# Dilated and sliding attention into a squared-ReLU layer: when keys, queries and values are turned and copied on the way to the next row

## The chip, the cores and the metric

The kernel runs on one core of one Trainium2 chip. The metric is the device time of one execution in microseconds (us), lower is better. Before the change it is 310.36 us, the median of three runs (309.91 to 311.45).

The engines that matter: PE (matrix multiplies; PEld are its weight loads), DVE (vector), ACT (activations and copies), POOL (casts, and one queue that issues transfers), SP (a queue that only issues transfers). Each engine, and each issuing queue, takes its instructions in program order; they meet through semaphores.

## The reference

`B, H, S, D = 8, 8, 576, 64`. Attention over 8 batch rows, 4 heads with a sliding window of 32, 4 heads with a dilated window (32 keys, every fourth), then a two-layer network with relu squared:

```python
    scores = scale * np.matmul(q, k.transpose(0, 1, 3, 2))
    mask_plain = (rel >= 0) & (rel < window)
    mask_dil = (rel >= 0) & (rel < window * dilation) & (rel % dilation == 0)
    attn = softmax of scores under the mask of the head
    x = np.matmul(attn, v) as (B * S, H * D)
    h = x @ w_in          # 4608 x 512 by 512 x 2048
    g = maximum(h, 0) ** 2
    out = g @ w_out       # 2048 x 512, float32
```

## The kernel before

Everything is in float16 on chip with float32 sums. The 4608 tokens are 8 batch rows of 576 (the attention's unit, called row b below) and 9 chunks of 512 (the network's unit, called chunk c). All order is written out by hand (`tc.manual_schedule()`): an engine executes in the order in which the Python code emits.

**The network as filler.** `moe_gen(c)` is a generator; each `yield` stands after a few matmuls. `mm1_gen` makes 16 tiles `ph` of `x @ w_in` (four matmuls of 512 columns each, line 298), ACT takes relu into `rt` (line 321), DVE squares into `g` (line 322). For chunks above 1, `sum_of_g` (lines 331, 332) and line 406 prepare sums and differences of `g` on DVE, and `mm2_strassen_gen` does the second product with seven half-size products instead of eight. Its bank `A` (tile `pa`) is used four times in turn; after each use ACT copies it out (`take`, line 391), and the next product into `A` has to wait for that copy. Outputs leave by SP (line 397). `pump(n)` advances the generator by n yields, so the attention code of row b, with `pump` between its steps, is woven into the matmuls of chunk b-1.

**Attention of one row.** `attn_scores` makes scores of the sliding heads (`s_sliding`, tiles `ps`, from `QKTp`) and of the dilated heads (`s_dilated`, tiles `pz`, from `QKTd`), with exp on ACT (line 563) and the mask on DVE (line 564). `av_sliding` (tiles `pav`, three steps `mp`) multiplies with the values `vp`, `av_dilated` (tiles `paw`, steps t, a) with `vd`; DVE normalizes into `xs` and `xd` (lines 605, 610). The result goes transposed into `xT`: for rows 0 to 3 by PE and ACT (`x_sliding`, `x_dilated`, lines 657, 675); for rows 4 to 7 (`attn_values_by_dma`) by transposing transfers on SP: `xT<-xs` (line 680), and `yd<-xd` (line 687, t = 0 and 1, called yd_0 and yd_1 here) which ACT then copies into `xT` (line 675, `x_from`).

**What row b+1 needs, made during row b.**
- sliding q and k: loaded by POOL into `ns` (line 112); DVE copies them into token order, `nr` (line 120); SP writes `nr` to DRAM as `dp` (line 217, two halves); SP transposes `dp` into `QKTp` (line 225, k first, then q). `turn` is `nr` and `dp` together.
- dilated q and k: POOL writes them to DRAM as `dd` (line 207); SP transposes into `QKTd` (line 229).
- values: SP loads `sv` (sliding, line 132) and `sd` (dilated, line 137); POOL casts them into `vp` (line 169) and `vd` (line 177).
- the overlap: blocks of values need the tail of the block before in their first partitions. `halo_sliding` (line 184) and `halo_dilated` (line 189) do it on ACT for rows 0 to 2; `halo_sliding_by_dma` (line 194) and `halo_dilated_by_dma` (line 197) do it on SP for rows 3 to 7. The name in the profile is `vp<-vp` and `vd<-vd`.
- `after_transposes` (line 235, tile `seen`) holds POOL's loads for the row after until the last transpose has landed; line 893 does the same with yd_1 ahead of the casts into `vp`.

**The loops.** Row 0 runs alone, with matmuls whose result nobody reads (`fill_gen`, line 507) in its waits; it ends at line 814. Row 1 runs inside the second product of chunk 0 (lines 820 to 836). Then `for b in range(2, 4)` (line 842) and `for b in range(4, B)` (line 867).

Of the kernel before, what the change touches and what calls it, by code (L numbers as in the profile page):

```python
# [17 lines left out]
def kernel(  # L18
# [106 lines left out]
    def load_sliding_v(b):  # L125
        vv = v[b, 0:HH].rearrange("h (m p) d -> p h m d", p=QB)
        if b == 0:
            for m in range(NB):
                nc.sync.dma_start(out=sv[PADP:P, :, m, :], in_=vv[:, :, m, :])
        else:  # L130
            for h in (0, 2):
                nc.sync.dma_start(out=sv[PADP:P, h : h + 2], in_=vv[:, h : h + 2])  # L132

    def load_dilated_v(b, eng):
        vv = v[b, HH:H].rearrange("h (i c) d -> i h (c d)", c=DIL)
        for t in range(2):
            eng.dma_start(out=sd[P - QD[t] : P, t, :, :], in_=vv[Q0D[t] : Q0D[t] + QD[t]])  # L137
# [55 lines left out]
    def halo_sliding_by_dma(b):  # L193
        nc.sync.dma_start(out=vp[b % 2][0:PADP, 1:NB], in_=vp[b % 2][P - PADP : P, 0 : NB - 1])
# [4 lines left out]
    def cast_v(b):  # L199
        cast_sliding_v(b)  # L200
        cast_dilated_v(b)
# [22 lines left out]
        for i in (1, 0):  # L224
            nc.sync.dma_start_transpose(out=QKTp[b % 2][:, i, :, PADP:], in_=dp[i])

    def transpose_dilated(b, dd):
        for i in (1, 0):
            nc.sync.dma_start_transpose(out=QKTd[b % 2][:, i, :, KPAD:], in_=dd[i])


# [271 lines left out]
    def fill_gen():  # L503
        for n in range(1000):
# [2 lines left out]
                nc.tensor.matmul(pf, ident, maskp[:, 0:TOKC], start=True, stop=True)  # L507
            yield

    pending: list = []  # L510

    def pump(n):
        for _ in range(n):
            while pending:
                try:
                    next(pending[0])
                    break
                except StopIteration:
                    pending.pop(0)
# [142 lines left out]
    def x_dilated(b, t, xs, wide):  # L662
        py = pt(f"py{b}_{t}", wide)
        w = QD[t]
        for r in range(DIL):
            x = xs[1][t][:, r].rearrange("p h d -> p (h d)")
            for c in range(2):
                o = w * (2 * r + c)
                nc.tensor.transpose(py[:, o : o + w], x[:, P * c : P * (c + 1)], ident[0:w, 0:w])
        x_from(b, t, py[:, 0 : 8 * w].rearrange("x (r c i) -> x r c i", r=DIL, c=2))  # L670
# [14 lines left out]
    def x_dilated_by_dma(b, t, xs):  # L685
        y = yp.tile([P, DIL, 2, QD[t]], FP16, name=f"yd{b}_{t}", tag=f"yd{t}")
        nc.sync.dma_start_transpose(
            out=y.rearrange("x r c i -> x (r c) i"), in_=xs[1][t].rearrange("p r h d -> p (r h d)")
        )
        return y  # L690

    def attn_scores(b, gap, less=0, hooks={}):
        for hp in range(2):
            s_sliding(b, hp)
            if hp in hooks:
                hooks[hp]()
            pump(gap)
        for g in range(2):
            s_dilated(b, g)
            if 2 + g in hooks:  # L700
                hooks[2 + g]()
            if g and b < 3:
                halo_sliding(b, 0)
            pump(gap - less)

    def attn_values(b, gap, wide=False, then=None):
        xs = x_tiles(b)
        for mp in range(3):
            av_sliding(b, mp, xs)
            if b < 3:  # L710
                if mp < 2:
                    halo_sliding(b, mp + 1)
                else:
                    halo_dilated(b, 0)
            if then and b == 2 and mp == 2:
                then()
            pump(gap)
        x_sliding(b, 0, xs, wide)
        if b < 3:
            halo_dilated(b, 2)  # L720
        pump(gap)
        av_dilated(b, 0, 0, xs)
        if then and b == 1:
            then()
        pump(gap)
        x_sliding(b, 1, xs, wide)
        pump(gap)
        av_dilated(b, 0, 1, xs)
        pump(gap)
        for a in range(2):  # L730
            av_dilated(b, 1, a, xs)
            pump(gap)
        x_dilated(b, 0, xs, wide)
        pump(gap)
        x_dilated(b, 1, xs, wide)

    def attn_values_by_dma(b, then):
        xs = x_tiles(b)
        for mp in range(3):
            av_sliding(b, mp, xs)  # L740
            if mp == 1:
                then[0]()
            pump(3)
        x_sliding_by_dma(b, xs)
        ys = []
        for t in range(2):
            for a in range(2):
                av_dilated(b, t, a, xs)
                pump(4 + 2 * (a > t))
            ys.append(x_dilated_by_dma(b, t, xs))  # L750
            then[1 + t](ys[t])
        pump(6)
        x_from(b, 0, ys[0])
        pump(7)
        x_from(b, 1, ys[1])
# [55 lines left out]
    av_dilated(0, 1, 1, xs)  # L811
    begun.append(mm1_begin(0, 1))
    x_dilated(0, 0, xs, False)
    x_dilated(0, 1, xs, False)


    g0 = hidden(0)
# [8 lines left out]
    for a in range(2):  # L826
        t_dilated(1, m, a, True)
        pump(2)
    attn_scores(1, 2, 1)
    dp = []  # L830
    attn_values(1, 1, True, lambda: dp.append(keep_sliding_qk(2, by_token(2, ns))))
    pump(1000)
# [2 lines left out]
    leave_first()  # L835
    load_v(2)


    def turn(b, n):
        return keep_sliding_qk(b, by_token(b, n))  # L840

    for b in range(2, 4):
        pending.append(moe_gen(b - 1))
        nxt = b + 1
        after_transposes(b)
        ns = load_sliding_qk(nxt)
        if b == 2:
            cast_v(b)
        dd = keep_dilated_qk(nxt)
        if b == 3:  # L850
            halo_sliding_by_dma(b)
            halo_dilated_by_dma(b)

        def turn_and_load():
            dp = turn(nxt, ns)
            load_sliding_v(nxt)
            load_dilated_v(nxt, nc.sync)
            transpose_sliding(nxt, dp)
            transpose_dilated(nxt, dd)
            cast_v(nxt)  # L860

        pump(22 if b == 2 else 12)
        attn_scores(b, 4, 0, {3: turn_and_load} if b == 3 else {})
        attn_values(b, b, False, turn_and_load)
        pump(1000)

    for b in range(4, B):
        pending.append(moe_gen(b - 1))
        nxt = b + 1
        if nxt < B:  # L870
            after_transposes(b)
            ns = load_sliding_qk(nxt)
            dd = keep_dilated_qk(nxt)
        if b > 4:
            cast_dilated_v(b)
        halo_sliding_by_dma(b)
        halo_dilated_by_dma(b)
        dps = []

        def copied():  # L880
            if nxt < B:
                dps.append(turn(nxt, ns))

        def first(y):
            if nxt < B:
                load_sliding_v(nxt)

        def second(y):
            if nxt < B:
                transpose_sliding(nxt, dps[0])  # L890
                transpose_dilated(nxt, dd)
                load_dilated_v(nxt, nc.sync)
                nc.gpsimd.tensor_copy(seen, y[:, 0, 0, 0:1])
                cast_sliding_v(nxt)

        pump(3)
        attn_scores(b, 3)
        attn_values_by_dma(b, (copied, first, second))
        pump(1000)
# [33 lines left out]
```

## Time and profile before

| | |
|---|---|
| runs, median of 3 | 310.36 us |
| the profiled execution | 309.19 us, of which 307.1 us lie between its first and last instruction (the span) |
| granted TensorE clock | 1.000 |
| PE busy | 286.5 us (93% of the span), 2762 matmuls |
| PE weight loads | 192.4 us (63%) |
| DVE | 210.1 us (68%) |
| ACT | 172.9 us (56%) |
| POOL | 64.2 us (21%) |
| SP's and ACT's transfer queue (q1) | 68832 packets, 32.96 MB, 51.9% of 16 engines' span |
| POOL's transfer queue (q0) | 8752 packets, 13.63 MB, 26.1% |

PE is busy nearly throughout, so the time is the matmuls plus PE's waits. A row of the timeline gives start, duration, engine, line, operation, and the number of instructions merged. `SPq` means the queue of SP issuing a transfer; the row's duration is that of the issue, and the landing is another, later time.

### The profile page before, as it was taken

Reading aid. Unit: us, or ns where it says so; the run is one execution under the profiler, and the core shown is the slowest. Engines: PE = TensorE matmul, PEld = TensorE weight load, DVE = VectorE, ACT = ScalarE, POOL = GpSimd, SP = SyncE. Lnnn points to the kernel's source line nnn. Section 1 sums busy time; section 2 is a strip of 40 time slices with the busy share of each in tenths; the row PEclk is TensorE's granted clock in tenths of the full one; section 3 lists DMA queues with packets and bytes.
Section 4 is the critical chain, followed back from the end, with each engine's and each line's share of the span. In section 5 each row is a group of like instructions: output and inputs, shape, how many; then the busy total and the mean of one; then the engine's idle time right before and its main releaser. Section 6 shows DMA issues by size and latency. Waiting matters only on the chain.

```text
span 307.1 us, 6899 instructions
## 1 busy us (share of the span) xinstructions
PE 286.5 (93%) x2762; PEld 192.4 (63%) x2762; DVE 210.1 (68%) x434; ACT 172.9 (56%) x293; POOL 64.2 (21%) x112
## 2 busy tenths in 40 slices
PE   1788998999999899999998999799989999999994
PEld 1345554555554468656887987458745875785584
DVE  7684447758843798489759984999398934834652
ACT  2766648668745863595457636763486446425620
POOL 4481027002704503310027002700230000000000
PEclk9999999999999999999999999999999999999999
DMA  7899998799599999995799979997983231003004
GB/s 116 187 204 213 208 173 152 157 215 221 119 211 176 242 191 187 258 187 120 127 171 260 220 126 188 267 189 131 158 252 22 45 111 40 2 1 139 0 1 138
DMA packets 77616, 47.03 MB, mean 153 GB/s; under 512 B 58480, under 2 KB 69232, under 8 KB 77584
## 3 DMA queue, kind: packets, MB, share of 16 engines
q1 hardware_dynamic: 68832, 32.96, 51.9%
q0 software_dynamic: 8752, 13.63, 26.1%
q8 instruction: 21, 0.34, 0.5%
q14 instruction: 11, 0.09, 0.1%
HBM read 36.70 MB, written 16.52 MB: 173 GB/s over the span
## 4 chain that ended last, share of the span: by engine, by line
PE 72%; DMA 12%; DVE 6%; SPq 3%; ACT 3%; issue 2%; POOL 0%; DVEq 0%; POOLq 0%
PE ph L298 32%; PE pa L375 15%; PE pb L375 7%; DMA vp<-vp 6%; PE po L441 6%; DMA QKTp<-dp 4%; PE pc L375 4%; PE paw L638 2%; PE pav L622 2%; DMA QKTd<-dd 1%; PE ps L573 1%; DMA sv<-in_v_dram 1%; ACT AT L563 1%; SPq L137 1%; SPq L132 1%
## 5 line engine op out<-in xcount | busy, mean ns | idle before, releaser
L298 PE MATMUL ph<-xT,wi 128*128 128x512 f16 (+1 forms) x640 | 134.2, 359 | 0.7 <-ACT xT L675 0.7
L321 ACT ACTIVATE rt<-ph 128x512 f16<-128x512 f32 x144 | 86.2, 608 | 47.5 <-PE ph L298 46.4
L298 PEld LDWEIGHTS <-wi 128*128 128x128 f16 x640 | 68.2, 114 | 45.9 <-issue 0.6
L322 DVE TENSOR_TENSOR g<-rt 128x512 f16<-128x512 f16 x144 | 63.4, 450 | 39.6 <-ACT rt L321 38.1
L375 PEld LDWEIGHTS <-g 128*128 128x128 f16 x448 | 43.3, 98 | 6.1
L375 PEld LDWEIGHTS <-gs 128*128 128x128 f16 x336 | 32.1, 98 | 4.0 <-DVE gs L332 0.3
L441 PE MATMUL po<-wo,g 128*128 128x512 f16 x128 | 33.1, 379 | 0.0
L402 DVE TENSOR_TENSOR ov<-pb,ov 128x512 f32<-128x512 f32 x14 | 9.7, 691 | 30.8 <-PE pb L375 17.4
L375 PE MATMUL pa<-wt,gs 128*128 128x256 f16 x224 | 27.2, 273 | 0.0
L375 PE MATMUL pb<-wt,g 128*128 128x256 f16 x224 | 27.1, 273 | 0.0
L169 POOL CAST vp<-sv 128x512 f16<-128x512 f32 x24 | 15.2, 664 | 53.4 <-DMA sv<-in_v_dram 39.5
L391 ACT COPY ov<-pa 128x512 f32<-128x512 f32 x14 | 8.2, 586 | 30.7 <-PE pa L375 30.7
L177 POOL CAST vd<-sd 128x512 f16<-128x512 f32 (+1 forms) x32 | 22.1, 717 | 11.4 <-PE ph L298 8.0
L610 DVE TENSOR_TENSOR xd<-paw,rcp_d 80x512 f16<-80x512 f32 (+1 forms) x32 | 21.9, 685 | 1.1
L563 ACT ACTIVATE AT<-pz 128x576 f16<-128x576 f32 x32 | 19.7, 694 | 1.2 <-PE pz L592 1.1
L563 ACT ACTIVATE AT<-ps 128x576 f16<-128x576 f32 x32 | 19.2, 657 | 2.2 <-PE ps L573 1.8
L564 DVE TENSOR_TENSOR AT<-AT,maskd 128x576 f16<-128x576 f16 x32 | 18.4, 604 | 1.8 <-ACT AT L563 0.7
L564 DVE TENSOR_TENSOR AT<-AT,maskp 128x576 f16<-128x576 f16 x32 | 15.5, 492 | 5.9 <-ACT AT L563 4.2
L391 ACT COPY ou<-pa 128x512 f32<-128x512 f32 x14 | 8.2, 586 | 15.8 <-PE pa L375 15.7
L610 DVE TENSOR_TENSOR xs<-pav,rcp_p 96x512 f16<-96x512 f32 x24 | 16.5, 687 | 0.8
L622 PEld LDWEIGHTS <-AT 128*128 128x128 f16 x192 | 9.3, 98 | 10.8 <-issue 6.0
L441 PEld LDWEIGHTS <-g 128*128 128x128 f16 x128 | 10.4, 98 | 8.3
(80 smaller groups left out, 276.7 us busy)
## 6 DMA issues: line engine op xcount, KB each, us to landing
sv<-in_v_dram SPq DMA_DIRECT2D x14, 288.0 KB, 5.3
dp<-nr SPq DMA_DIRECT2D x12, 288.0 KB, 4.0
out_dram<-ou SPq DMA_DIRECT2D x6, 512.0 KB, 4.0
out_dram<-ov SPq DMA_DIRECT2D x6, 512.0 KB, 4.7
sd<-in_v_dram SPq DMA_DIRECT2D x8, 320.0 KB, 6.2
ns<-in_k_dram POOLq DMA_DIRECT2D x8, 288.0 KB, 6.3
ns<-in_q_dram POOLq DMA_DIRECT2D x8, 288.0 KB, 7.8
sd<-in_v_dram SPq DMA_DIRECT2D x8, 256.0 KB, 6.0
```

The lines of the kernel that those rows point to most:

```text
L169: nc.gpsimd.tensor_copy(vp[b % 2][:, m : m + 2, :, 0:D], sv[:, :, m : m + 2, :].rearrange("p h m d -> p m h d"))
L177: nc.gpsimd.tensor_copy(vd[b % 2][p0:P, t, c : c + 2, :, 0:D], sd[p0:P, t, :, D * c : D * (c + 2)].rearrange("p h (c d) -> p c h d", d=D),)
L298: nc.tensor.matmul(ph[:, t0:t1], wi4[ffc // 4][:, dmk, :, ffc % 4], xT[:, dmk, x0 : x0 + t1 - t0], start=(dmk == 0 and t0 == 0), stop=(dmk ...
L321: nc.scalar.activation(rt, ph[:], ACTF.Relu)
L322: nc.vector.tensor_mul(g[:, ffc, :], rt, rt)
L375: nc.tensor.matmul(banks[bank][:, t], a(k, t), b(k), start=(new and t == 0 and k == 0), stop=(k == HF - 1), skip_group_check=True,)
L391: nc.scalar.copy(ot, banks[A])
L441: nc.tensor.matmul(po, g[:, ffc, t * P : (t + 1) * P], wo[ffc // 4][:, ffc % 4, :], start=(ffc == 0), stop=(ffc == NFF - 1),)
L563: nc.scalar.activation(AT[:, u, 0:UW], ps[:, :, 0 : UW // 2], ACTF.Exp, scale=scale)
L564: nc.vector.tensor_mul(AT[:, u, 0:UW], AT[:, u, 0:UW], mask)
L610: nc.vector.tensor_tensor(out=x, in0=pv, in1=rb, op=ALU.mult)
L622: nc.tensor.matmul(pav[:, i, h * (D + 2) : h * (D + 2) + D + 1], AT[:, 2 * (h // 2) + m // 3, off : off + P], vp[b % 2][:, m, h, 0 : D + 1 ...
```

## The change

Five edits, in the order of the kernel's run:

1. **Row 0's end.** A new `fill_wide(n)` emits two 512-column matmuls into a tile that nobody reads; it is called after `x_dilated(0, 0)` and after `x_dilated(0, 1)`.
2. **Row 1's first overlap copy** (`halo_sliding(1, 0)`, on ACT) is emitted after the second pair of sliding scores instead of after the last dilated scores. For row 2 it stays where it was.
3. **Row 3 (made during row 2).** `turn` is called after step `mp == 1` of `av_sliding` instead of `mp == 2`. On SP the loads of `sd` stand behind all transposes instead of ahead of them. The overlap copy `vp<-vp` of row 3 stands between the two `QKTd` transposes. The casts into `vd` move to the next loop turn, behind POOL's loads. `pump(12)` becomes `pump(9)`.
4. **Row 4 (made during row 3).** `sv` is still loaded at the last dilated scores, but `turn` and all that follows it moves from there to behind `av_dilated(3, 0, 0)`. SP's order after it is as for row 3.
5. **Rows 5 to 7 (made during rows 4 to 6).** `turn` moves from behind `av_sliding` step `mp == 1` to behind both steps of `av_dilated(b, 0, .)`, ahead of the issue of yd_0. The overlap copy `vp<-vp` moves from the next loop turn (behind `sd` and the two outputs on SP) to between the two `QKTd` transposes; the loads of `sd` stand behind the second.

Orders that follow from it, for rows 4 to 6. SP before: dp, dp, xT, xT, yd_0, sv, sv, yd_1, QKTp, QKTp, QKTd, QKTd, sd, sd, output, output, vp<-vp, vd<-vd. SP after: xT, xT, dp, dp, yd_0, sv, sv, yd_1, QKTp, QKTp, QKTd (k), vp<-vp, QKTd (q), sd, sd, output, output, vd<-vd. On DVE `nr` stood between the normalizing of `pav` 1 and 2; after the change it stands behind line 406, ahead of the normalizing of `paw` (1, 0). The order of PE's instructions in rows 4 to 7 is the same in both.

```diff
@@ -224,8 +224,8 @@
         for i in (1, 0):
             nc.sync.dma_start_transpose(out=QKTp[b % 2][:, i, :, PADP:], in_=dp[i])
 
-    def transpose_dilated(b, dd):
-        for i in (1, 0):
+    def transpose_dilated(b, dd, sides=(1, 0)):
+        for i in sides:
             nc.sync.dma_start_transpose(out=QKTd[b % 2][:, i, :, KPAD:], in_=dd[i])
 
 
@@ -507,6 +507,11 @@
                 nc.tensor.matmul(pf, ident, maskp[:, 0:TOKC], start=True, stop=True)
             yield
 
+    def fill_wide(n):
+        pf = pa(f"pw{n}")
+        for _ in range(2):
+            nc.tensor.matmul(pf[:, 0], ident, maskp[:, 0:TOKC], start=True, stop=True)
+
     pending: list = []
 
     def pump(n):
@@ -699,7 +704,7 @@
             s_dilated(b, g)
             if 2 + g in hooks:
                 hooks[2 + g]()
-            if g and b < 3:
+            if g and b == 2:
                 halo_sliding(b, 0)
             pump(gap - less)
 
@@ -712,7 +717,7 @@
                     halo_sliding(b, mp + 1)
                 else:
                     halo_dilated(b, 0)
-            if then and b == 2 and mp == 2:
+            if then and b == 2 and mp == 1:
                 then()
             pump(gap)
         x_sliding(b, 0, xs, wide)
@@ -720,7 +725,7 @@
             halo_dilated(b, 2)
         pump(gap)
         av_dilated(b, 0, 0, xs)
-        if then and b == 1:
+        if then and b != 2:
             then()
         pump(gap)
         x_sliding(b, 1, xs, wide)
@@ -738,8 +743,6 @@
         xs = x_tiles(b)
         for mp in range(3):
             av_sliding(b, mp, xs)
-            if mp == 1:
-                then[0]()
             pump(3)
         x_sliding_by_dma(b, xs)
         ys = []
@@ -747,6 +750,8 @@
             for a in range(2):
                 av_dilated(b, t, a, xs)
                 pump(4 + 2 * (a > t))
+            if t == 0:
+                then[0]()
             ys.append(x_dilated_by_dma(b, t, xs))
             then[1 + t](ys[t])
         pump(6)
@@ -811,7 +816,9 @@
     av_dilated(0, 1, 1, xs)
     begun.append(mm1_begin(0, 1))
     x_dilated(0, 0, xs, False)
+    fill_wide(0)
     x_dilated(0, 1, xs, False)
+    fill_wide(1)
 
 
     g0 = hidden(0)
@@ -826,7 +833,7 @@
     for a in range(2):
         t_dilated(1, m, a, True)
         pump(2)
-    attn_scores(1, 2, 1)
+    attn_scores(1, 2, 1, {1: lambda: halo_sliding(1, 0)})
     dp = []
     attn_values(1, 1, True, lambda: dp.append(keep_sliding_qk(2, by_token(2, ns))))
     pump(1000)
@@ -835,6 +842,12 @@
     leave_first()
     load_v(2)
 
+
+    def transpose_and_load(b, dd):
+        transpose_dilated(b, dd, (1,))
+        halo_sliding_by_dma(b)
+        transpose_dilated(b, dd, (0,))
+        load_dilated_v(b, nc.sync)
 
     def turn(b, n):
         return keep_sliding_qk(b, by_token(b, n))
@@ -848,19 +861,19 @@
             cast_v(b)
         dd = keep_dilated_qk(nxt)
         if b == 3:
-            halo_sliding_by_dma(b)
+            cast_dilated_v(b)
             halo_dilated_by_dma(b)
 
         def turn_and_load():
             dp = turn(nxt, ns)
-            load_sliding_v(nxt)
-            load_dilated_v(nxt, nc.sync)
+            if b == 2:
+                load_sliding_v(nxt)
             transpose_sliding(nxt, dp)
-            transpose_dilated(nxt, dd)
-            cast_v(nxt)
-
-        pump(22 if b == 2 else 12)
-        attn_scores(b, 4, 0, {3: turn_and_load} if b == 3 else {})
+            cast_sliding_v(nxt)
+            transpose_and_load(nxt, dd)
+
+        pump(22 if b == 2 else 9)
+        attn_scores(b, 4, 0, {3: lambda: load_sliding_v(nxt)} if b == 3 else {})
         attn_values(b, b, False, turn_and_load)
         pump(1000)
 
@@ -871,9 +884,7 @@
             after_transposes(b)
             ns = load_sliding_qk(nxt)
             dd = keep_dilated_qk(nxt)
-        if b > 4:
-            cast_dilated_v(b)
-        halo_sliding_by_dma(b)
+        cast_dilated_v(b)
         halo_dilated_by_dma(b)
         dps = []
 
@@ -888,10 +899,9 @@
         def second(y):
             if nxt < B:
                 transpose_sliding(nxt, dps[0])
-                transpose_dilated(nxt, dd)
-                load_dilated_v(nxt, nc.sync)
                 nc.gpsimd.tensor_copy(seen, y[:, 0, 0, 0:1])
                 cast_sliding_v(nxt)
+                transpose_and_load(nxt, dd)
 
         pump(3)
         attn_scores(b, 3)
```

## The prediction

> **What bounds the kernel now.** First the chain that ended last, on the page, for what sets the time:
>
> ```profile
> PE 72%; DMA 12%; DVE 6%; SPq 3%; ACT 3%; issue 2%; POOL 0%; DVEq 0%; POOLq 0%
> ```
>
> PE sets it, but 12% of the chain are transfers, so some arrive late. Then PE's own waits (us in total, times, longest), since only those can be won:
>
> ```profile
> PE pav L622 <- DMA vp<-vp: 3.8, 3, 1.6
> ...
> PE ps L573 <- DMA QKTp<-dp: 1.0, 1, 1.0
> PE pav L622 <- ACT vp L184: 0.7, 2, 0.5
> ```
>
> The timeline of each gives what PE lost, measured between the starts of matmuls less their usual pitch: 1.45, 1.79 and 1.01 us in rows 5, 6, 7 for the overlap copy `vp<-vp`; 1.18 for `QKTp` of row 3, 0.30 for that of row 7; 0.71 in row 1 for ACT's overlap copy. Together 6.4 us: more than that the edits can't win, apart from row 0. Last, the stage that edit 5 touches, row 4 (the rows 5 and 6 have the same order):
>
> ```profile
> 144.31 1.04 PE L375 MATMUL pa<-wo,g 128*128 128x256 f16 x8
> 144.55 0.60 ACT L321 ACTIVATE rt<-ph 128x512 f16<-128x512 f32 x1 [0.31 <-PE ph L298]
> ...
> 145.66 1.81 SPq L687 DMA_TRANSPOSE yd<-xd  x1
> ...
> 147.06 0.69 DVE L332 TENSOR_TENSOR gs<-gs,g 128x1024 f16<-128x1024 f16 x1
> ...
> 147.67 1.22 DVE L406 TENSOR_TENSOR g<-g 128x2048 f16<-128x2048 f16 x1
> ...
> 149.99 1.30 ACT L675 COPY xT<-yd 128x640 f16<-128x640 f16 x1
> ...
> 152.68 1.04 PE L375 MATMUL pc<-wo,g 128*128 128x256 f16 x8
> 152.88 0.59 ACT L391 COPY ov<-pa 128x512 f32<-128x512 f32 x1 [1.58 <-PE pa L375]
> ...
> 153.55 1.91 PE L375 MATMUL pa<-wo,gs 128*128 128x256 f16 x16
> ```
>
> The last lines show a place without slack. ACT copies bank `A` out from 152.88 to 153.47, and the next product into `A` starts at 153.55. Whatever holds ACT before 152.88 holds PE. ACT's instruction ahead of it is the copy of yd_0 into `xT`, 1.31 us: it may start at 151.5 at the latest. Before the change yd_0 had landed at 148.81 (2.7 us of slack); in row 5 180.54 against 182.9, in row 6 211.31 against 214.5.
>
> **Edit 5, the gain.** `vp<-vp` now waits only for the casts and stands ahead of 576 KB of `sd` and 1 MB of output. By row 5's times: yd_1 lands, POOL's `seen` 0.19 and three casts 1.72 us follow, SP issues in 0.7, the landing took 3.3 us where little stood ahead (row 4, 128.68 to 132.01). Even if yd_1 comes 3 us later than before (153.3), that is 156.3 + 1.9 + 0.7 + 3.3 = 162.2, and PE asks for it at 165.7. The three waits go: -4.25 us. If one casting came too late after all and the largest wait stayed, 2.5 would be won.
>
> **Edit 5, the price.** `nr` costs DVE 0.75 us wherever it is, with PE not waiting for DVE. But it now stands behind line 406, which ends at 148.89 (row 4), 180.34 (row 5), 211.85 (row 6); and dp waits for `nr`, and yd_0 stands behind dp on SP, though `xd` is ready at 145.64. The sum for row 4: `nr` ends at 148.89 + 0.75 = 149.64, or 0.7 earlier if DVE, freed of `nr` above, is no longer behind: the floor is relu of the last `ph` at 145.15, then 0.45 + 0.72 + 0.72 + 1.22 + 0.75 (rows 322, 331, 332, 406, 120) = 149.0. I take 149.3. Two issues of dp take 1.14, so yd_0 is issued at 150.5 instead of 145.66. From issue to landing yd took 2.7 to 4.3 us, median 2.9; with two 288 KB writes directly ahead I take 3.3: it lands at 153.8. ACT's copy ends at 155.1, bank `A` is out at 155.8, and PE goes on at 155.9 instead of 153.55: 2.3 us. The two ends: with 149.0 and 2.7 it is 1.4 us; with 149.64 and 4.3 it is 3.6. Rows 5 and 6 have the same distances (line 406 ends 4.66, 4.61 and 4.66 us before that product starts in rows 4, 5, 6). Three rows: +6.9 us, 4.2 to 10.8. Row 7 prepares no row and pays nothing.
>
> [...] In this trace transposes that were issued right behind the dp copies took 2.6 to 5.4 us to land, and those without dp ahead (row 7) 3.6 and 4.1, which does not separate them. [...]
>
> What else is queued behind dp: sv, yd_1, `QKTp`, `QKTd`. In row 4: yd_1 issued at 153.0, `QKTp` q at 155.6; it took 3.73, 4.75 and 5.38 us to land in the three rows. That is 159.3 for row 5, where PE now asks at 158.45 + 2.3 = 160.75; rows 6 and 7 come out at 0 to 0.5 us late. `QKTd` q stands behind the overlap copy, which waits for POOL: about 158.8 plus 3.75 to 5.0 = 162.6 to 163.8, asked for at 162.04 + 2.3. I take +0.3 for all these, 0 to 2. `sd` comes some 2 us later, but the casts into `vd` start behind POOL's loads anyway, and `vd<-vd` has until `paw` (1, 0), 5.5 us after `paw` (0, 0).
>
> **Edit 3.** `nr` starts behind `xs` 1 (82.6) instead of `xs` 2, 1.25 us sooner; `sd`'s two issues (89.09 to 92.40) no longer stand ahead of `QKTp`. dp's second half lands 1.25 sooner, at 90.45; `QKTp` q is issued there instead of at 94.07, and with the 6.8 us that it took before, `sd` ahead of it, it lands at 97.2 at the latest. PE, three yields of 0.43 us sooner, asks at 99.72 - 1.29 = 98.4. The wait of 1.18 goes; I take -1.0 (0 to -1.2). The cover is 1.2 us; if dp is that much slower, the old wait is back.
>
> **Edit 4.** All counted from the start of `paw` (3, 0, 0). The last `ph` ends at -2.4; relu takes 0.85 with its delay, then DVE rows 322, 331, 332, 406, 605, 610, 120 stand in line: 0.42 + 0.69 + 0.69 + 1.22 + 0.20 + 0.69 + 0.75 = 4.66, so `nr` ends at 3.1, or 4.0 with the normalizing of `pav` 2 still ahead, which I take. dp's second half is issued at 4.6 and lands 4.2 later (112.14 to 116.33), at 8.8; `QKTp` q then needs 3.7 to 5.4 (rows 5 to 7): 12.5 to 14.2. PE's work up to the scores of row 4, in the new order, is 92 x 0.109 + 6 x 0.216 + 4 x 0.26 + 0.7 = 13.06 us. No slack is left: +0.3 (0 to +1.5). Rows 0 to 3 use no yd, so ACT isn't held here. 0.44 us for DVE before `pav` 2 (113.21) stays: the sums of `g` are in the way as `nr` was.
>
> **Edit 2.** ACT's copy (0.41 us) moves ahead of the exps, where ACT had 0.27 us idle (49.38 to 49.65); exps end 0.15 later, and `pav` waits for the second copy instead (52.6 for 52.96): -0.3, between -0.7 and +0.2.
>
> **Edit 1.** Four matmuls at 0.216 us, 0.43 per call. The second stands in PE's wait for ACT, 24.99 to 25.67, and is covered; the first shifts half of `py` 1 by under 0.1 us: +0.1. The granted clock is 1.00 between 24.0 and 26.5 and the first 60 matmuls afterwards run at 0.218 us each, so nothing shows a cold PE that they could warm. If all of PE's 0.84 us wait there were won, -0.8; uncovered calls +0.9.
>
> **Sum.** -4.25 + 6.9 + 0.3 - 1.0 + 0.3 - 0.3 + 0.1 = +2.05. The profiled execution took 309.19 us (307.1 of span, 2.1 around it), so 311.2; the median of the runs is 1.2 above it, so 312.4. What this kernel's measurement can tell from no change is about 0.5%, 1.55 us: 308.8 to 311.9.
>
> **Rivals.**
> - *ACT isn't held long (faster).* Place: ACT's copy of yd_0. If it costs the 1.4 us of the floor (4.2 in all), and edits 1 to 3 win all that they can (-0.8 - 0.7 - 1.2), the sum is -4.25 + 4.2 - 2.7 = -2.75: 307.6. For it: DVE's backlog after 139.25 is made by `nr` itself. Against: even the floor of 149.0 leaves yd_0 only 1.4 us from issue to 151.5, and no yd landed in under 2.7. It decides (sum below -1.55) where the three rows cost less than 3.3 us together with all else as I take it (-4.25 - 0.6), or less than 5.4 with edits 1 to 3 at their best (-4.25 - 2.7). Chance 0.2.
> - *Gain and price cancel.* 1.5 to 2 us a row (4.5 to 6), the rest as taken: -0.35 to +1.15, about 310.8. The same rows speak for it. Chance 0.2.
> - *The next row waits as well.* dp's second half takes 6.6 us, as it did for row 3 (85.14 to 91.70). Then it lands at 149.9 + 6.6 = 156.5, `QKTp` q is issued 0.9 later than 155.6 in rows 5 to 7, and row 4's scores wait their 1.5: 2.05 + 2.7 + 1.2 = +5.95, 316.3. For it: DMA engines are 0.89 to 1.12 busy in these stretches. Against: POOL's loads that made row 3 slow lie elsewhere in rows 4 to 6. Chance 0.1.
> - *The fills warm PE.* Only row 0, -0.8 at most; the clock row speaks against it; within the ranges above.
>
> Forecast 0.5: slower, 312.4 (its own range 311 to 315). Low end: the faster rival's 307.6 is cut where some 0.1 of chance lies below, 308.6; high end 315.4, short of 316.3, with another 0.1 above. Faster 0.2; within 0.5% 0.2; slower 0.5 + 0.1 = 0.6.
>
> **What would show it.** Right: no `pav <- DMA vp<-vp` among PE's waits; a new wait of ACT's line 680 for `yd<-xd` of 2 to 4 us ahead of the `ov` copy in rows 4, 5, 6, and PE's last product into `pa` waiting for ACT some 2.3 us, three times; SP idle between the second xT and dp. Wrong, if yd_0 lands within 1 us of dp, or `nr` comes out ahead of line 406 in time. If ps of row 3 still waits for `QKTp`, edit 3 was mis-sized; if ps of row 4 does, edit 4.

## The result: slower by 3%, three waits for bank A and a half clock behind each

The changed kernel takes 318.86 us (median of 4 runs, 318.27 to 322.94), the kernel before 310.65 us on the same chip (4 runs). The ratio is 1.029, 95% interval 1.020 to 1.038. The profiled execution took 318.8 us with a span of 317.0 us, against 307.1 before. The prediction was 312.4 us, with a range of 308.6 to 315.4: the direction was right, the time too low by 6.5 us.

From line 507 on, a line stands 5 further down in the changed kernel: 675 is 680 there, 687 is 692. First the chain that ended last, on the page of the changed kernel:

```profile
PE 63%; DVE 19%; ACT 7%; DMA 6%; issue 3%; SPq 1%; POOL 0%; DVEq 0%; POOLq 0%
```

Transfers have fallen from 12% to 6%, and DVE has risen from 6% to 19%: transfers no longer end last so often, the DVE work ahead of them does. PE's waits (us in total, times, longest):

```profile
PE pa L375 <- ACT ov L391: 9.0, 3, 3.2
...
PE pav L627 <- DVE rcp_p L610: 0.7, 1, 0.7
...
PE pav L627 <- DVE xs L615: 0.5, 1, 0.5
...
PE pav L627 <- ACT vp L184: 0.2, 1, 0.2
```

`vp<-vp` (3.8 us) and `QKTp<-dp` (1.0 us) are gone from the list. In their place stands one line that was not there before: three waits for ACT's copy out of bank `A`. The timeline of row 4 in the changed kernel shows how one of them comes about (start, duration, engine, line, operation; in brackets the idle time before it and what ended it):

```profile
147.65 1.22 DVE L406 TENSOR_TENSOR g<-g 128x2048 f16<-128x2048 f16 x1
...
148.79 0.75 DVE L120 COPY nr<-ns 128x2304 f16<-128x2304 f16 x1
...
149.57 1.14 SPq L217 DMA_DIRECT2D dp<-nr  x2
...
150.76 2.62 SPq L692 DMA_TRANSPOSE yd<-xd  x1
...
152.60 1.04 PE L375 MATMUL pc<-wo,g 128*128 128x256 f16 x8
...
155.02 1.26 ACT L680 COPY xT<-yd 128x640 f16<-128x640 f16 x1 [5.12 <-DMA yd<-xd]
156.19 0.58 ACT L391 COPY ov<-pa 128x512 f32<-128x512 f32 x1
...
156.82 2.95 PE L375 MATMUL pa<-wo,gs 128*128 128x256 f16 x16 [3.18 <-ACT ov L391]
```

Read it downwards: `nr` stands behind line 406, dp behind `nr`, yd_0 behind dp on SP. The trace has dp's second half landing at 154.37 and yd_0 at 154.99. ACT waits 5.12 us for yd_0, because in program order its copy into `xT` stands ahead of the copy out of bank `A`. PE has finished `pc` at 153.6 and can't start the next product into `A` before 156.82.

The last line holds a second cost. The same 16 matmuls took 1.91 us before; here 2.95. The granted clock by stage (stretch, its length, busy time of PE, PEld, DVE, ACT, POOL, then the clock, DMA share and GB/s):

```profile
127.00:158.00 31.00, 27.82 (x267) 18.49 (x266) 24.10 (x48) 16.29 (x28) 5.74 (x9) 0.99 0.88 172
158.00:190.00 32.00, 30.58 (x345) 27.36 (x344) 22.61 (x47) 16.41 (x29) 7.60 (x13) 0.95 0.90 170
190.00:222.00 32.00, 30.52 (x280) 20.73 (x280) 23.99 (x48) 17.63 (x30) 7.35 (x13) 0.95 0.92 176
222.00:254.00 32.00, 29.06 (x267) 19.13 (x266) 21.93 (x46) 18.09 (x31) 4.70 (x8) 0.95 0.76 143
```

Before the change the clock was 1.00 here. The trace's clock records give three spells of half clock, each 3.41 us long, beginning at 157.5, 191.6 and 225.8, where PE's waits end (156.8, 191.5 and 226.0). Half of a spell's length, 1.7 us, is taken below as what PE loses in it (an estimate from the 3.41 us and the clock of 0.5).

The account, from the starts of the first scores of each row (lengths of waits are the distance between the starts of matmuls less their usual pitch, as in the prediction):

| stretch | before, us | after, us | difference | what makes it |
|---|---|---|---|---|
| to row 0's scores | 8.17 | 8.45 | +0.28 | the loads at the start |
| rows 0 to 2, to row 2's scores | 63.15 | 63.61 | +0.46 | edits 1 and 2 |
| row 2 to row 4's scores | 57.34 | 56.38 | -0.96 | wait for `QKTp` of row 3 (1.18) gone |
| row 4 to 5 | 29.79 | 34.94 | +5.15 | wait 3.34, half clock 1.7 |
| row 5 to 6 | 31.39 | 34.65 | +3.26 | wait 3.07, half clock 1.7, `vp<-vp` -1.45 |
| row 6 to 7 | 31.76 | 34.40 | +2.64 | wait 3.10, half clock 1.7, `vp<-vp` -1.79, `QKTp` -0.30 |
| row 7 to PE's end | 81.64 | 80.71 | -0.93 | `vp<-vp` -1.01 |

The sum is +9.9 us, the difference of the two spans. The medians lie 8.2 us apart: the profiled execution of the kernel before was 1.2 to 1.5 us faster than its medians. The 1.7 us of half clock are half of a spell; the three rows, less the waits in them, leave 1.8, 1.7 and 1.6 us for it.

Rows 0 and 1 differ more between executions than edits 1 and 2 were expected to change them. Row 0, from its first scores to those of row 1, took 37.2 to 38.6 us in the eleven profiles with edit 1 (here 38.55), 38.3 and 38.9 in the two without; row 1 took 24.4 to 26.1 us in the ten profiles with edit 2 (here 25.06), 24.8 in all three without. So edit 2 made row 1 longer in eight of ten. Nine of the eleven rows 0 with edit 1 took less than 38.0 us, so edit 1 may win something; the account above, from one pair of executions, can't show it.

### The profile page after: what moved, and what is told of

Same layout as the page of the kernel before. It is cut to its first block, busy times and chain, and to the rows that moved or that the text cites. A ratio compares the mean times of both kernels' runs of the same rounds, so it can differ in the third digit from the quotient of the medians.

```text
span 317.0 us, 6894 instructions
## 1 busy us (share of the span) xinstructions
PE 293.7 (93%) x2766; PEld 195.3 (62%) x2766; DVE 211.4 (67%) x434; ACT 172.8 (55%) x293; POOL 65.5 (21%) x112
## 4 chain that ended last, share of the span: by engine, by line
PE 63%; DVE 19%; ACT 7%; DMA 6%; issue 3%; SPq 1%; POOL 0%; DVEq 0%; POOLq 0%
PE ph L298 26%; PE pa L375 12%; PE po L441 8%; PE pb L375 6%; DVE g L322 5%; DVE AT L569 4%; DMA yd<-xd 4%; ACT AT L568 3%; DVE xs L615 3%; PE pc L375 2%; ACT rt L321 2%; PE paw L643 2%; DVE gs L331 2%; DMA ns<-in_q_dram 2%; PE ps L578 2%
## 5 line engine op out<-in xcount | busy, mean ns | idle before, releaser
L322 DVE TENSOR_TENSOR g<-rt 128x512 f16<-128x512 f16 x144 | 62.4, 446 | 36.8 <-ACT rt L321 35.4
L375 PEld LDWEIGHTS <-gs 128*128 128x128 f16 x336 | 33.8, 103 | 15.7 <-issue 9.5
L375 PE MATMUL pa<-wo,gs 128*128 128x256 f16 x112 | 17.7, 323 | 9.0 <-ACT ov L391 9.0
L177 POOL CAST vd<-sd 128x512 f16<-128x512 f32 (+1 forms) x32 | 23.1, 750 | 10.2 <-DMA sd<-in_v_dram 9.2
L569 DVE TENSOR_TENSOR AT<-AT,maskd 128x576 f16<-128x576 f16 x32 | 20.8, 683 | 1.7 <-ACT AT L568 0.7
L680 ACT COPY xT<-yd 128x640 f16<-128x640 f16 (+1 forms) x8 | 9.4, 1177 | 22.7 <-DMA yd<-xd 22.7
L391 ACT COPY ov<-pa 128x512 f32<-128x512 f32 x14 | 8.2, 585 | 24.8 <-PE pa L375 24.8
```

The source lines that it names most:

```text
L177: nc.gpsimd.tensor_copy(vd[b % 2][p0:P, t, c : c + 2, :, 0:D], sd[p0:P, t, :, D * c : D * (c + 2)].rearrange("p h (c d) -> p c h d", d=D),)
L322: nc.vector.tensor_mul(g[:, ffc, :], rt, rt)
L375: nc.tensor.matmul(banks[bank][:, t], a(k, t), b(k), start=(new and t == 0 and k == 0), stop=(k == HF - 1), skip_group_check=True,)
L569: nc.vector.tensor_mul(AT[:, u, 0:UW], AT[:, u, 0:UW], mask)
L680: nc.scalar.copy(o, y.rearrange("x r c i -> x c i r"))
```

## The experiments

Each ratio below is the time over that of the kernel before, measured on the same chip, with its 95% interval.

The theory to begin with: the late copy (edit 5's move of `nr` and dp) costs what the profile shows, 9.5 us of waits and 5.1 of half clock; with the copy elsewhere the other edits would win. The rivals: the order on SP alone is at fault; the half clock is a by-product that costs nothing; the rest of the change costs something itself.

### e1_copy_early: the changed kernel with the copy back where it was, rows 5 to 7

```diff
             av_sliding(b, mp, xs)
+            if mp == 1:
+                then[0]()
             pump(3)
...
-            if t == 0:
-                then[0]()
```

> The changed kernel with one part undone: for rows 5 to 7 the copy in token order and dp stand again behind pav step 1, ahead of the xT transposes. Theory (the cost is all made by the late copy: three waits of PE for bank A of 3.34, 3.07 and 3.10 us and three spells of 3.4 us at half clock behind them, 1.7 us lost in each): no wait of PE for ACT's ov copy, clock 1.00 throughout, the three waits for vp<-vp stay away, so 318.9 - 9.5 - 5.1 = 304.3, at most 306. Rival (the overlap copy between the QKTd transposes holds SP and makes the row late): clock below 1.00 in places, 314 or more.

Measured: 311.07 us (10 runs), ratio 1.0037, interval 0.999 to 1.0085. The waits for bank `A`, the three spells of half clock (the granted clock is 0.997, against 0.984 in the changed kernel) and the waits for `vp<-vp` are all gone, so nearly all of the 3% is the late copy. But the gain that was expected isn't there either. Among the waits of this run:

```profile
PE paw L643 <- DVE xs L615: 4.4, 3, 2.3
```

And DVE's timeline in row 4:

```profile
138.73 0.69 DVE L615 TENSOR_TENSOR xs<-pav,rcp_p 96x512 f16<-96x512 f32 x1
140.53 0.76 DVE L120 COPY nr<-ns 128x2304 f16<-128x2304 f16 x1 [1.11 <-DMA ns<-in_q_dram]
...
141.77 0.69 DVE L615 TENSOR_TENSOR xs<-pav,rcp_p 96x512 f16<-96x512 f32 x1
```

DVE stands idle for `ns`, and `xs` of the next step stands behind `nr`; PE waits for that `xs` 0.94, 2.43 and 1.55 us in the three rows. `ns` landed at 140.45, 173.82 and 206.05, `nr` began at 140.53, 173.85 and 206.13. Before the change `ns` landed at 136.75 in row 4, 2.5 us ahead of `nr`; in rows 5 and 6 it was on the edge already (170.67 and 201.93 against 170.70 and 202.21). POOL holds the loads of `ns` until `QKTd` q has landed (`seen`, line 235), and edits 3 to 5 put the overlap copy, which waits for POOL's casts, ahead of `QKTd` q. Counted from the first scores of rows 4, 5 and 6, `QKTd` q landed 2.4, 0.5 and 0.4 us later than before the change and the loads took 2.1, 1.4 and 0.6 us longer, so `ns` landed 4.4, 1.9 and 1.0 us later. So the sooner overlap copy isn't free: it delays the loads of the row after. In rows 5 and 6, though, more of the lateness comes from the loads taking longer, the cause of which was not followed. In the changed kernel this is hidden, since `nr` comes late there anyway.

### e2_yd_first: the changed kernel with the copy right behind the issue of yd_0

```diff
-            if t == 0:
-                then[0]()
             ys.append(x_dilated_by_dma(b, t, xs))
+            if t == 0:
+                then[0]()
```

> The changed kernel with one order on SP exchanged: yd_0 is issued ahead of the copy in token order and dp; the copy keeps its late place on DVE, behind line 406. Theory (it is dp ahead of yd_0 in SP's order that holds ACT): yd_0 lands about 148.6 in row 4's time, no wait for bank A, clock 1.00; QKTp is later than in the kernel with the early copy, 0 to 1.6 us a row: 305 to 309. Rival (the late place on DVE alone makes the cost, by delaying what stands behind it): 314 or more, with the wait for bank A still there.

Measured: 318.37 us, ratio 1.0215, interval 1.018 to 1.025. The gain that was expected stays away. yd_0 now landed 2.7 us after its issue (144.86 to 147.52), and the wait for bank `A` is gone. What stood behind dp is late instead:

```profile
PE ps L578 <- DMA QKTp<-dp: 4.8, 3, 3.1
PE ph L298 <- ACT xT L680: 4.4, 2, 2.6
```

yd_1, behind dp and `sv`, took 6.0 us to land (152.43 to 158.43), `QKTp` q landed at 160.74 and row 5's scores began at 160.78. Three spells of half clock stand behind these waits too (at 161.9, 196.0 and 230.2). The order on SP chooses which wait appears; the lateness of the copy, whose place on DVE is the same in both, is the cause.

### e3_fill_gap: the changed kernel, with matmuls in the wait

```diff
-        pump(7)
+        pump(4)
+        if b < 7:
+            fill_wide(b, 14)
+        pump(3)
```

14 unused matmuls of 512 columns (0.22 us each) stand ahead of the product that waits for bank `A` in rows 4 to 6.

> The changed kernel with 14 matmuls of 512 columns that nobody reads (14 x 0.216 = 3.0 us) ahead of the last product into bank A in rows 4 to 6, where PE waits 3.1 to 3.3 us for ACT. They take none of the wait away. Theory (the half clock follows from PE standing idle for most of a window): clock 1.00 throughout, 318.9 - 3 x 1.7 = 313.8. Rival (the half clock has another cause, or costs nothing): clock 0.98 to 0.99 and 318 to 319.5. If the matmuls came on top of the wait: 328.

Measured: 320.35 us, ratio 1.029, interval 1.0247 to 1.0332: the same as without the fill. The clock stayed at 1.00, so it is the idle time that brings the half clock. Yet the time is no shorter:

```profile
PE ps L578 <- DMA QKTp<-dp: 3.0, 2, 1.9
PE pa L375 <- ACT ov L391: 1.4, 2, 1.2
```

In the changed kernel `QKTp` of row 5 landed at 163.00 and its scores began at 163.38: had PE come sooner, by more than 0.38 us, it would have waited for `QKTp`. That is what happens here (1.31 us in row 5, 2.03 in row 6). In rows 6 and 7 of the changed kernel `QKTp` landed 1.06 and 0.09 us ahead of its scores. So without the half clock, and with `QKTp` no sooner, that kernel could have won some 1.5 us (an estimate, the sum of these three distances), not 5.1. In this run's profiled execution the stretch from row 0's first scores to PE's end is 1.2 us shorter than in the changed kernel (303.5 against 304.7), but row 0 began 2.0 us later (10.42 against 8.45), which was not followed up. Nor was it why in row 6 the transpose landed 1.9 us later than in the changed kernel (198.88 against 196.98): some 0.75 us of it are a later issue, the rest a longer transfer. Whether the half clock has a price of its own couldn't be told from this run; the last two settle it.

### e4_only_late: the kernel before, with only the copy moved

```diff
-            if mp == 1:
-                then[0]()
             pump(3)
...
+            if t == 0:
+                then[0]()
             ys.append(x_dilated_by_dma(b, t, xs))
```

> The kernel before with one part of the change alone: the copy in token order of rows 5 to 7 stands behind both steps of the dilated values of t = 0, ahead of yd_0; the overlap copy and all else as before. Theory: waits for bank A of 3.1 to 3.3 us in rows 4, 5, 6, each with a spell of half clock, 3 x 4.9 = +14.6; the waits for vp<-vp (4.25) stay in part, since both SP and PE are later by nearly the same: 322 to 326. Rival (the late copy is harmless without the rest of the change): 309 to 313.

Measured: 329.05 us, ratio 1.054, interval 1.047 to 1.0605, clock 0.984.

```profile
PE pa L375 <- ACT ov L391: 8.7, 3, 3.0
PE pav L622 <- DMA vp<-vp: 5.4, 3, 2.5
```

That is above the 322 to 326 that were expected. Alone the late copy costs more than in the whole change: the waits for bank `A` are nearly the same (8.7 us against 9.0), and those for `vp<-vp`, still behind the outputs on SP, are longer in two rows of three (2.70, 1.68 and 1.51 us, against 1.45, 1.79 and 1.01 before). One of its three spells of half clock stands behind such a wait (at 173.7). Going from here to the whole change takes the ratio from 1.054 to 1.029: where the copy is late, the sooner overlap copy and the rest do earn something.

### e5_copy_mid: the changed kernel with the copy one step of PE sooner

```diff
                 av_dilated(b, t, a, xs)
+                if t == 0 and a == 0:
+                    then[0]()
                 pump(4 + 2 * (a > t))
-            if t == 0:
-                then[0]()
```

> The changed kernel with the copy in token order of rows 5 to 7 behind the first dilated step (t = 0, a = 0) instead of behind both. On DVE it then stands ahead of the squares 12 to 15, the sums and line 406, some 5 us sooner than in the change, and some 4 us later than before it. Theory (the early copy waits for ns, which the overlap copy made late; the late copy makes yd_0 and QKTp late; between them there is room for both): no wait for bank A, no wait of DVE for ns, clock 1.00, no wait for vp<-vp: 305 to 307. Rival (any place behind the sliding values makes yd_0 late): waits for bank A again, 312 or more.

Measured: 306.84 us (10 runs, 305.64 to 308.79) against 310.04 on the same chip, ratio 0.9939, interval 0.9907 to 0.9972. It beats both kernels, the one before by 0.6%. Its timeline of row 4:

```profile
142.76 0.75 DVE L120 COPY nr<-ns 128x2304 f16<-128x2304 f16 x1
...
143.93 1.17 SPq L217 DMA_DIRECT2D dp<-nr  x2
...
145.19 2.59 SPq L692 DMA_TRANSPOSE yd<-xd  x1
...
149.51 1.30 ACT L680 COPY xT<-yd 128x640 f16<-128x640 f16 x1 [0.22 <-DMA yd<-xd]
...
152.20 0.58 ACT L391 COPY ov<-pa 128x512 f32<-128x512 f32 x1 [1.39 <-PE pa L375]
...
152.88 1.91 PE L375 MATMUL pa<-wo,gs 128*128 128x256 f16 x16
```

`nr` now begins 2.5 us behind the landing of `ns` (140.22) and stands ahead of the sums that end with line 406. yd_0 is issued 5.6 us sooner than in the changed kernel, ACT idles 1.39 us before the copy out of bank `A` instead of holding it up, and PE goes on at once. Neither `vp<-vp` nor `QKTp` is waited for in this execution, though `QKTp` of row 5 landed only 0.16 us ahead of its scores (157.62 and 157.78), and the clock is 1.00. What is left in these rows is a short wait for DVE's sums:

```profile
PE pa L375 <- DVE gs L332: 1.4, 3, 0.5
```

e1 and e6, where `nr` also stands ahead of these sums, have the same three waits. The changed kernel, where it stands behind them, has none, but neither has the kernel before, where it stands ahead; what makes them was not tested. Between two places that each cost much lies one that costs little.

### e6_overlap_behind: e1 with the overlap copy behind both `QKTd` transposes

```diff
-        transpose_dilated(b, dd, (1,))
+        transpose_dilated(b, dd)
         halo_sliding_by_dma(b)
-        transpose_dilated(b, dd, (0,))
         load_dilated_v(b, nc.sync)
```

> The kernel with the early copy, and the overlap copy behind both QKTd transposes instead of between them (still ahead of sd and the outputs). Theory (in the run with the early copy, the overlap copy and its wait for POOL held back QKTd q, so the loads of ns that wait for it came 2 us later, and the copy on DVE waited for ns): ns lands as before the change, the waits of PE for DVE's xs (4.4 us) fall to 1 or less, and vp<-vp lands in time: 305 to 307.5. Rival (ns is late for another reason, such as traffic): waits stay, 310 to 312.

Measured: 309.43 us, ratio 0.9976, interval 0.9936 to 1.0017. PE's waits for `xs` fell from 0.94, 2.43 and 1.55 us to 0.61, 0.53 and 0.60, and the overlap copy is still in time. DVE still waits for `ns`:

```profile
DVE nr L120 <- DMA ns<-in_q_dram: 2.6, 3, 1.0
```

The mechanism of e1 holds (the wait for `QKTd` q moves the loads of `ns`), but more than half of the gain that was expected stays away: the time is 1.6 us below e1's, on another chip, and the intervals of the two ratios overlap. At this early place the copy is on the edge of the loads.

### e7_rows_0_to_4: the kernel before with edits 1 to 4 alone

Edit 5's two moves are taken back, so rows 5 to 7 are prepared as before (the edit as against the changed kernel):

```diff
             av_sliding(b, mp, xs)
+            if mp == 1:
+                then[0]()
...
-            if t == 0:
-                then[0]()
...
+        if b > 4:
+            halo_sliding_by_dma(b)
         halo_dilated_by_dma(b)
...
                 transpose_sliding(nxt, dps[0])
+                transpose_dilated(nxt, dd)
+                load_dilated_v(nxt, nc.sync)
...
-                transpose_and_load(nxt, dd)
```

> The kernel before with edits 1 to 4 alone (fills of row 0, overlap copy of row 1, rows 3 and 4); rows 5 to 7 are made as before. Theory of the prediction: -1.0 for QKTp of row 3, +0.3, -0.3 and +0.1, so 0.9 below the kernel before. From the trace of the change (row 4's scores start only 0.2 us sooner than before) it is nearer -0.2 to -0.5. Rival (edits 1 to 4 cost as much as edit 5 does): 3 or more above it.

Measured: 312.74 us, ratio 1.0085, interval 1.0039 to 1.0131: the wrong sign. Row 4's scores begin at 127.29 instead of 128.66, so rows 0 to 3 do win 1.4 us. But row 4 is turned later, `ns` of row 5 lands at 139.97 instead of 136.75, and the gain goes back: 2.1 us in row 4, most of it in small waits for DVE (0.38, 0.79 and 0.64 us), and 1.7 us in row 5, where the old wait is 3.14 us instead of 1.45:

```profile
PE pav L627 <- DMA vp<-vp: 5.4, 3, 3.0
```

Alone, edits 1 to 4 lose: what they win in rows 0 to 3 is only kept if the transfers of rows 4 and 5 follow.

### e8_k_side: e1 with `seen` reading the k half of `QKTd`

```diff
-        nc.gpsimd.tensor_copy(seen, QKTd[b % 2][:, 0, 1, KPAD : KPAD + 1])
+        nc.gpsimd.tensor_copy(seen, QKTd[b % 2][:, 1, 1, KPAD : KPAD + 1])
```

> The kernel with the early copy, with one thing changed: POOL's loads of the row after wait for the k half of QKTd, which SP issues ahead of the overlap copy, not for the q half behind it. Theory (DVE's copy in token order waited for ns, and ns for QKTd q): ns lands about 2 us sooner, PE's waits for xs (0.94, 2.43 and 1.55) go, 305.5 to 307.5. Rival (the loads then only slow the transfers next to them by as much): 310 to 312.

Measured: 308.58 us, ratio 0.9976, interval 0.993 to 1.0022.

```profile
PE pav L627 <- POOL vp L169: 1.8, 1, 1.8
...
PE paw L643 <- DVE xs L615: 0.6, 2, 0.3
```

The waits for `xs` fall from 4.4 us to 0.6, so the gate on `QKTd` q is what made `ns` too late. The time, at 308.58 us, lies between the theory (305.5 to 307.5) and the rival (310 to 312). A new wait of 2.0 us in row 2, for casts on POOL whose `sv` landed at 81.1, takes much of that back; the gate serves every row, so the edit reaches row 2 as well. How it makes that `sv` late was not followed.

### e9_mid_no_halo: e5 with edit 2 undone

```diff
-            if g and b == 2:
+            if g and b < 3:
                 halo_sliding(b, 0)
...
-    attn_scores(1, 2, 1, {1: lambda: halo_sliding(1, 0)})
+    attn_scores(1, 2, 1)
```

> The kernel with the copy behind the first dilated product (306.84 us), with edit 2 undone: row 1's sliding overlap values are turned after the last dilated scores again. Theory: the 1.2 us for which the first product with v of row 1 waits for rcp_p is the price of edit 2, since the halo evictions stand ahead of rcp_p on VectorE; it goes, and the time is about 305.7 to 306.2. Rival: what edit 2 moved comes back as a wait further on in row 1 (the overlap product paw or the first vp), and the time stays within 0.3 of 306.8.

Measured: 307.04 us (306.63 to 307.51), ratio 0.989, interval 0.982 to 0.996: the rival, within 0.3 us of e5. In the profile row 1's wait for `rcp_p` (1.19 us) is gone, the one for ACT's overlap copy is back (0.70 us), and row 1 takes 24.80 us instead of 25.39; row 0 took 1.1 us longer in that execution. Edit 2 costs some 0.6 us in row 1 by these two traces, and nothing that the medians can show. (The copies of edit 2 run on ACT, line 184, not on VectorE as the expectation has it.)

### e10_idle and e11_idle_filled: the price of the half clock by itself

In e5 nothing is late behind bank `A`. Six more copies on ACT there hold the bank for 3.5 us; e11 also has the 14 unused matmuls of e3.

```diff
         o22 = take(lower, 1)
+        for _ in range(6 if 2 < c < 6 else 0):
+            nc.scalar.copy(o22, banks[A])
```

> The kernel with the copy behind the first dilated product (306.84 us), with six more copies of bank A into the same output tile on ScalarE behind the third product of A, in rows 4, 5 and 6 (some 0.58 us each): TensorE then waits for bank A about 3.1 us in each row, as in the changed kernel, but nothing in the chain of the copy in token order is late. Theory (the half clock costs what its matmuls show): three waits of 3.1 us and three spells of half clock of 3.4 us, 1.7 us lost in each: 306.8 + 9.3 + 5.1 = about 321. Rival (a wait of this length does not bring the half clock by itself, or the loss is covered): about 316, with a clock of 1.0 or with waits further on that shrink.

> The same with the six copies, and with 14 unused matmuls of 512 columns (some 0.22 us each, 3.0 us in all) ahead of the product that waits for bank A in rows 4, 5 and 6. Theory: TensorE's waits are filled, the clock stays at 1.0, and the time is 306.8 + 9.3 = about 316, 5 us below the run with the idle waits. Rival: as in the changed kernel with the same fill, the time equals that of the run without fill, whatever the clock.

Measured: 321.28 us (320.53 to 321.5) with the idle wait, ratio 1.034, interval 1.025 to 1.043; 316.58 us (316.13 to 317.25) with it filled, ratio 1.020, interval 1.012 to 1.027. 4.7 us lie between them, 5 were expected. PE's timeline of e10 has the product behind the wait in rows 4, 5 and 6:

```profile
157.46 3.57 PE L375 MATMUL pa<-wo,gs 128*128 128x256 f16 x16 [3.51 <-ACT ov L423]
...
194.07 3.38 PE L375 MATMUL pa<-wo,gs 128*128 128x256 f16 x16 [3.51 <-ACT ov L423]
...
229.36 1.91 PE L375 MATMUL pa<-wo,gs 128*128 128x256 f16 x16 [3.51 <-ACT ov L423]
```

Three waits of the same 3.51 us: behind two of them the 16 matmuls run at about half speed, behind the third at full speed. The rows agree (distance between the first scores of neighbouring rows, us):

| | e5 | e10, idle | e11, filled | e10 - e11 | half clock in e10 |
|---|---|---|---|---|---|
| row 4 to 5 | 30.49 | 36.97 | 34.28 | 2.69 | 6.83 us, from 156.2 |
| row 5 to 6 | 30.88 | 35.39 | 33.91 | 1.48 | 3.41 us, from 193.7 |
| row 6 to 7 | 30.58 | 33.81 | 33.81 | 0.00 | none |

With the fill PE's waits for bank `A` shrink to 0.5 us a row, and the clock is 1.00 in all three stretches (128 to 162, 162 to 196, 196 to 230; 0.91, 0.95 and 0.98 in e10):

```profile
PE pa L375 <- ACT ov L423: 1.5, 3, 0.5
```

So the half clock is paid for where nothing later is late, and is mostly covered where something is (e3). That a fill keeps the clock up is shown in both kernels; that it wins time, in this one alone.

## Why the prediction was wrong

Term by term, from the table of stretches and the waits (us):

| term | predicted | measured |
|---|---|---|
| edit 5, waits for `vp<-vp` | -4.25 | -4.25 |
| edit 5, bank `A` waits for ACT | +6.9 | +9.5 |
| the same waits, half clock | not in the sum | +5.1 |
| transfers behind dp | +0.3 | -0.3 |
| edit 3 | -1.0 | -1.1 |
| edit 4 | +0.3 | +0.1 |
| edit 2 | -0.3 | +0.25 |
| edit 1 | +0.1 | +0.2 |
| sum | +2.05 | +9.5 |

Edits 3 and 4 are the stretches from row 2 to 3 and from 3 to 4, less three yields of 0.43 us by which PE's own order moved; the measured sum lacks 0.28 us of later start and some rounding.

**Right.** The place, the chain and the count: `nr` behind line 406, then dp, yd_0, ACT's copy, bank `A`, in three rows and not in row 7. `nr` ended at 149.54 (149.3 was taken), yd_0 was issued at 150.76 (150.5). The waits for `vp<-vp` and for row 3's `QKTp` went as the prediction says, and row 4's scores did not wait.

**The step that failed: the price of edit 5, by the time that yd_0 takes to land behind dp.** "From issue to landing yd took 2.7 to 4.3 us, median 2.9; with two 288 KB writes directly ahead I take 3.3." It took 4.2 us in all three rows, at the end of that range. This 0.9 and the 0.26 of the later issue in row 4 account, within 0.2 us, for the miss of the wait: 3.1 to 3.3 us where 2.3 were taken. In the three rows yd_0 landed 0.62 to 0.66 us behind dp's second half (154.99 after 154.37 in row 4, 189.66 after 189.04, 224.20 after 223.55). In e3, e4 and e5 it was 0.61 to 0.66 us in all nine rows, also where dp's second half itself took 4.76 us (e5, row 5) and 5.31 (e3, row 6): yd_0 then landed 2.2 and 2.7 us after its issue had ended, elsewhere 1.5 to 1.7. Without dp ahead, in e2, the same transfer took 2.7 to 3.0 us. The trace of before already pointed to such a landing right behind dp. The prediction compared how long transposes took and found that this "does not separate them"; compared by landing, the `xT` transposes that were issued right behind dp landed 0.81, 0.74 and 0.42 us behind dp's second half in rows 4 to 6, the last 5.4 us after its issue, where dp took 5.7. An estimate from these: dp's second half issued 0.6 us ahead of yd_0 (149.9 by the prediction's times), 4.15 us to its landing as in row 4 before, and 0.4 to 0.8 us more give yd_0 at 154.5 to 154.9 instead of 153.8, and a price of 3.0 to 3.4 us a row instead of 2.3.

**The term that was missing.** The price went as far as 3.6 us a row and counted PE's wait alone. It did not ask what an idle TensorE does to the clock, and the clock appears in the text only for row 0, where "nothing shows a cold PE". At 3.1 us a row the wait brought 1.7 us of half clock. With the waits for bank `A` as measured the prediction's sum is +4.65 us, on the 310.36 of before 315.0 us, still inside the range; with the half clock it is +9.75, 320.1 us, against 318.9 measured. The 5.1 us are what the half clock takes in this trace. They are not what the kernel would win without it: e3 keeps the clock at 1.00 and is no faster, because `QKTp`, behind dp as well, is late next. The prediction priced all that is queued behind dp at +0.3 us; with PE not held at bank `A`, e2 waits 4.8 us for `QKTp`. The profile of before couldn't show it: its clock is 1.00 in every stretch of these rows, and its longest wait of PE in rows 4 to 7 is 1.79 us.

**Edit 2** had the wrong sign, just outside its bounds (-0.7 to +0.2): row 1 got 0.25 us longer, and one of its products with v waits for `rcp_p`. That the early overlap copy delays the exps and masks ahead of `rcp_p` would fit the order on ACT and DVE; e9 shows only that this wait goes with the edit.

**The rivals.** "The next row waits as well" came nearest in time (316.3), but not by its mechanism: dp's second half took 4.25 us, not 6.6, and no scores waited for `QKTp`. That transfer did lie close, landing 0.38, 1.06 and 0.09 us ahead of the scores of rows 5, 6 and 7, and e2 and e3 show it as the next limit. The faster rival needed a price under 3.3 us; with the copy one step sooner, as in e5, the kernel is faster, by 0.6%.

**Open.** Why `QKTp` of row 6 landed late in e3, why the loads of `ns` took longer in e1, and what makes row 0 differ by more than 1 us from one profile to the next.

## What to carry to other kernels

When an edit makes TensorE idle for about 3 us at a stretch, price the wait and a spell of half clock behind it (here 3.2 + 1.7 us a row; in e10, behind three waits of 3.51 us, 2.7, 1.5 and 0), and ask what is late next before counting on a fill. A step that is moved on one in-order queue moves everything issued behind it, so look for the place between the two bounds, here behind the landing of `ns` and ahead of DVE's block of sums: in row 4 the copy began at 140.5 us in e1 (no gain), at 142.8 in e5 (0.6% faster than before) and at 148.8 in the changed kernel (3% slower). An edit that lands one transfer sooner can delay a gate that reads a later one: with the sooner overlap copy `QKTd` q and the loads of `ns` came later, and e1 had 4.9 us of new waits.

## What the runs showed of the hardware

**The half clock came on a grid of 3.413 us, and not behind every long wait.** All spells that begin before PE's work ends last 3.41 us or twice that, and in each kernel their starts lie whole multiples of 3.413 us apart (34.13 us, ten steps, between the three in the changed kernel). Counting TensorE's idle time within the 3.41 us ahead of a spell, from the gaps between the matmul records, gives 2.73, 2.91 and 2.68 us in the changed kernel, 2.29, 1.90 and 2.61 in e2, 3.00, 2.50 and 2.21 in e4, 2.21 and 3.14 in e10. Windows of 3.41 us on that grid that held 1.78 (e4), 1.87 (e1) and 1.99 us (e10) were followed by the full clock. In e10's double spell the first window at half clock held 1.29 us of idle time. So in these runs 1.90 us of idle time in such a window was followed by a spell once and 1.99 us once was not. In e10 the wait of 3.51 us in row 6 fell across two windows, 1.99 and 1.51 us in them, and no spell followed. e4 shows the same: its wait of 2.85 us for bank `A` in row 5 fell across two windows (1.78 and 1.07) and brought no spell.
